# A larger fixed part for VectorE's instructions in the plan of the first attention, later inverses, and ScalarE's copies of the output projection behind the last exponential

## Chip, cores and metric

One core of one Trainium2 chip. The metric is the device time of one execution in microseconds (us); each kernel's time is the median of its runs.

## What is computed

Four layers follow one another on x of 2048 x 640 (float32): attention, a state-space convolution, attention again, the convolution again, each with a layer norm in front and the input added behind. Both attentions have the same weights, with 32 heads of 20 channels. Cut to what matters:

```python
def _A_ref(x, wqkv, wo):                     # H = 32, D = 640, S = 2048
    q, k, v = split(x @ wqkv)                # 32 heads of 20
    p = softmax(einsum("bhqd,bhkd->bhqk", q, k) * Dh ** -0.5)
    return merge(einsum("bhqk,bhkd->bhqd", p, v)) @ wo

def _B_ref(u, ...):                          # per channel, 128 states
    K = 2 Re(sum_n C[d, n] * exp(A[d, n] * dt[d] * pos))
    return causal_conv(u, K) + u * D_skip    # by FFT in the reference

x = x + _A_ref(layernorm(x)); x = x + _B_ref(layernorm(x))
x = x + _A_ref(layernorm(x)); x = x + _B_ref(layernorm(x))
```

## The kernel before

**Attention.** `attention` runs over 32 turns. A turn is a group g of four heads (8 groups) by a block qb of 512 queries (4 blocks), and it has 16 steps kt of 128 keys. In each step TensorE (PE) makes the scores of two pairs of heads (S, L858), ScalarE (ACT) takes their exponentials (pt, one instruction of 128 x 1024 for each pair, so 32 a turn and 1024 an attention), and `values` multiplies pt with V into two accumulators pa (L892). V has a column of ones, which gives the sums of the softmax. At the end of a turn VectorE (DVE) copies and adds pa to oc. PE needs that copy before it can write the next turn's pa. The sums of a block (number 4g + qb) go over DRAM: `sums` stores them (dn<-oc), `load` brings them back across all partitions (dr<-dn), `invert` takes 1/x on VectorE, `back` stores that (dn<-dr), and `spread` reads it for all rows (db<-dn). `scale` multiplies oc by db right behind the next turn's evacuation, and `store_block` writes the result (ot<-oc). These DMAs are issued by GpSimd (POOL).

**Work between the exponentials.** While the attention runs, PE and VectorE get other work. `jobs` is the projection of the next heads' q and k: units of 15 matrix products into the two banks m (L611), followed on VectorE by five instructions that `post` and its caller issue: qc (twice), sq, qhi, qlo. Two stores (qs or ks, on SP's queue) then send qhi and qlo to DRAM, from where `load_k` and `load_q` bring them into kop and qop, also on SP's queue. In the first attention there is also `kgen`, the filler: VectorE builds tables of the convolution's kernel K (expansions kpw, ktab, kwc, kwb, then products ka and kb), `contract` multiplies them on PE (m<-kb,ka, L329), VectorE empties that into ko, and kd<-ko stores it.

**What sets the order.** Instructions of an engine run in the order in which they are recorded, and `Plan` decides that order with modelled times for PE, ScalarE and VectorE. Every VectorE instruction is priced in `Ordered` (L77) at a fixed part of 0.07 us and one element per partition each 1/960 us. `weave` hands out filler as long as the planned time of VectorE is less than 0.2 us past that of PE. `emptied` plans when a bank is free, `slot` starts jobs by it, and `fill` does all of it once per exponential. A list `later` holds functions by planned time; the steps of a block's sums stand in it at fixed distances from the evacuation (L935), and with them the loads of the filler's powers (kpw<-wd). When filler and jobs are done, `end_jobs` frees their space and asks for the output weights wo and for x (SP); GpSimd splits the weights in two parts (woh and wol, L1169 and L1170).

**The end.** `out_proj` multiplies the stored blocks with wo, row tile by row tile. `Rows.split` copies a row tile to oh and VectorE takes the rest (ol). The first row tile's copy is VectorE's, the next ones are ScalarE's (CAST oh). `se.floor`, where it is set, ties ScalarE's later instructions behind a given one.

Of the kernel before, what the change touches and what calls it, by code (L numbers as in the profile page):

```python
# [50 lines left out]
class Plan:  # L51


    def __init__(self):
        self.pe = self.act = self.dve = 0.0
        self.keep = False

    def on_pe(self, cost, after=0.0):
        self.pe = max(self.pe, after) + cost
# [3 lines left out]
class Ordered:  # L63
# [5 lines left out]
    def __getattr__(self, name):  # L69
        f = getattr(self.engine, name)  # L70
        if name not in ("dma_start", "memset", "partition_all_reduce", "activation", "copy") and not self.count:
            return f

        def call(out, *a, **k):
            if self.count:
                big = a[0].shape if "reduce" in name else out.shape
                self.plan.dve = max(self.plan.dve, self.plan.pe - 0.9) + 0.07 + math.prod(big[1:]) / 960  # L77
            made = f(out, *a, **k)  # L78
            if self.plan.keep:
                self.last = self.tie(made, self.last)  # L80
            elif self.floor is not None:
                self.tie(made, self.floor)
            return made
        return call
# [3 lines left out]
def mha_s4d_kernel(ctx, tc, x_in, wqkv, wo, lar, aim, cr, ci, ldt, dsk,  # L88
                   c_e1, c_eb, c_f2, c_fa, c_sel, c_lv, c_id, c_sg, c_e16, c_f16, c_id16, c_dn, out, parts="asas", general=None):
    nc = tc.nc  # L90
    plan = Plan()
# [9 lines left out]
    se, ve, ge, sy = (Ordered(e, plan, tie, e is nc.vector) for e in (nc.scalar, nc.vector, nc.gpsimd, nc.sync))  # L101
# [87 lines left out]
    def chain(ins):  # L189
        last[0] = tie(ins, last[0])  # L190
# [208 lines left out]
    pend, slow = [], []  # L399
# [23 lines left out]
    def attention(x, stats):  # L423
        first_layer = stats is None
# [99 lines left out]
        sqs, outs, later, ends = [[], []], [], [], [0.0, 0.0]  # L524
# [318 lines left out]
        ends[:] = plan.pe, plan.pe  # L843
        sums_ = [plan.pe]
        se.last = ve.last = ge.last = sy.last = None
        plan.keep = True
        pp = c.enter_context(tc.tile_pool(name="pp", bufs=PB))
        ev = c.enter_context(tc.tile_pool(name="ev", bufs=2))
        ready, scaled, stored = [], [], {}
# [17 lines left out]
        def store_block(oc, blk):  # L867
            g, qb = divmod(blk, 4)
            for j in range(4):
                h = 4 * g + j  # L870
                ge.dma_start(ot[h * DH:(h + 1) * DH, 512 * qb:512 * qb + 512], oc[32 * j:32 * j + DH, :])
            stored[blk] = plan.pe

        def at_once(oc, blk):

            pb = pst("M", [P, 512], F32, tag="m0", name="m0")
            db = ev.tile([P, 512], F32, bufs=1, name="db")
            te.matmul(pb, dsel[0], oc, start=True, stop=True)
            ve.tensor_scalar_max(db, pb, 1e-30)
            ve.reciprocal(db, db)  # L880
            ve.tensor_mul(oc, oc, db)
            store_block(oc, blk)

        def values(qb, g, kt, pts, pa):

            V = Vt[g // 2 % 3]
            plan.on_pe(0.865)
            for r in range(2):
                rows = slice(64 * r, 64 * r + 64)
                for j in range(4):  # L890
                    h = 4 * (g % 2) + j
                    chain(te.matmul(pa[r][32 * j:32 * j + 32, :], V[rows, kt, VP * h:VP * h + 32],  # L892
                                    pts[j // 2][rows, 512 * (j % 2):512 * (j % 2) + 512],
                                    start=(kt == 0), stop=(kt == NI - 1), tile_position=(64 * r, 32 * j)))
            if kt == NI - 1:
                blk = 4 * g + qb
                oc = ev.tile([P, 512], F32, name="oc")
                dr = ev.tile([P, 16], F32, name="dr")
                db = []
                rows = dn[0, blk].rearrange("(j c) f -> j (c f)", j=4)  # L900
                plan.dve = max(plan.dve, plan.pe + 0.25)
                ve.tensor_copy(oc, pa[0])
                ve.tensor_add(oc, oc, pa[1])
                sums_[0] = plan.dve + 0.15
                while scaled:
                    scaled.pop(0)()
                if dsel and blk == NBK - 1:
                    later.append((plan.dve, lambda: at_once(oc, blk)))
                    return

                def sums():
                    for j in range(4):
                        ge.dma_start(rows[j:j + 1, :], oc[32 * j + DH:32 * j + DH + 1, :])

                def load():
                    ge.dma_start(dr, dn[0, blk])

                def invert():
                    ve.tensor_scalar_max(dr, dr, 1e-30)
                    ve.reciprocal(dr, dr)  # L920

                def back():
                    ge.dma_start(dn[1, blk], dr)

                def spread():
                    rows = dn[1, blk].rearrange("(j c) f -> j (c f)", j=4)
                    db.append(ev.tile([P, 512], F32, bufs=1, name="db"))
                    for j in range(4):
                        ge.dma_start(db[0][32 * j:32 * j + 32, :], rows[j:j + 1, :].to_broadcast([32, 512]))

                def scale():
                    ve.tensor_mul(oc, oc, db[0])
                    later.append((plan.dve + 0.3, lambda: store_block(oc, blk)))
                    later.sort(key=lambda e: e[0])
                later.extend((plan.dve + n, f) for n, f in (  # L935
                    (0.2, sums), (5.0, load), (10.0, invert), (11.0, back), (15.5, spread)))
                later.extend((plan.dve + n, lambda: slow and slow.pop(0)[1]()) for n in (18.0, 21.0, 24.0))
                if first_layer or g < H // 4 - 2:
                    scaled.append(scale)
                else:  # L940
                    later.append((plan.dve + 27.0, scale))
                later.sort(key=lambda e: e[0])
# [27 lines left out]
        def fill(j):  # L970

            if ready:
                t = max(ready[0][0] + 0.15, 0.0 if ready[0][3] else sums_[0])
                if t <= plan.pe + 0.1 or j and len(ready) > 2:
                    plan.on_pe(0.0, t)
                    values(*ready.pop(0)[1:])
            while slot(plan.act - 0.5):
                pass
            drain_later()
            weave()  # L980
# [146 lines left out]
        for r_ in ready:  # L1127
            values(*r_[1:])
# [11 lines left out]
            scaled.pop(0)()  # L1140
            drain_later(True)
        plan.keep = False
        se.floor = None if first_layer else se.last
        c.close()
        return *tail[:-1], rows, first

# [421 lines left out]
    def seq(x, general):  # L1568

        stats = None  # L1570
        for n in range(0, len(parts), 2):
            with ExitStack() as c:
                if general:
                    if stats is not None:
                        xpools.pop().__exit__(None, None, None)
                    attention_general(x)
                else:
                    x, wc, *tail = attention(x, stats)
                    rows = tail[2]
# [123 lines left out]
```

## Time and profile before

| | |
|---|---|
| median of 3 runs | 2681.47 us (2677.0 to 2681.95) |
| the profiled execution | 2680.85 us, span 2679.1 us |
| PE busy | 2530.0 us, 94% |
| ScalarE busy | 2368.7 us, 88% |
| VectorE busy | 1516.0 us, 57% |
| exponentials | 2048, each 1032 ns; they overlap |
| first exponential to the end of the last, first attention | 115.77 to 1101.84 us |
| the same, second attention | from 1491.2 us |

A row of the timeline has start and length in us, the engine, the line and operation, what is written <- what is read, the number of instructions, and in brackets the idle time in front with what ended it. The line L78 is the recording helper, so the tiles tell the instructions apart. SPq and POOLq rows are DMA issues. A row of stretches has the bounds, the length, and the busy time of PE, PE's weight loads, VectorE, ScalarE and GpSimd (with counts), then PE's granted clock, the DMA share and GB/s. A row of waits has who waited <- for whom: us in all, times, longest.

### The profile page before, as it was taken

The page shows a single profiled execution, that of the slowest core. Times are in us where ns is not written, and L with a number is a line of the kernel's source. Part 1 is how long each engine was busy: PE and PEld are TensorE (multiplying, and loading weights), DVE is VectorE, ACT ScalarE, POOL GpSimd, SP SyncE. Part 2 cuts the span into 40 slices and gives each one's busy share as a digit, 9 for nine tenths or more (in the row PEclk, how much of TensorE's full clock was granted, in tenths as well). Part 3 has the DMA queues.
Part 4 walks back from the last instruction along what each step waited for, and adds up shares of the span by engine and source line. Part 5 has one row for each costly group of instructions (what it writes and reads, how often), then busy time and mean ns, then how long its engine had stood idle before and what let it go on. Part 6 is the DMA issues. An engine that isn't in the chain of part 4 may idle for free.

```text
span 2679.1 us, 116332 instructions
## 1 busy us (share of the span) xinstructions
PE 2530.0 (94%) x51106; PEld 1425.0 (53%) x51106; DVE 1516.0 (57%) x3451; ACT 2368.7 (88%) x2793; POOL 827.7 (31%) x1256
## 2 busy tenths in 40 slices
PE   7899999999999998899998999999999998999898
PEld 3445444444444443678896444454444443444788
DVE  8687777886855994477776333232233221154865
ACT  7889999999999999676655799999999999999564
POOL 1123323333323334301672122222222222222376
PEclk9999999999999999999999999999999999999999
DMA  6513222322221224364542121121121113222465
GB/s 210 181 49 86 67 76 55 87 55 76 52 61 49 54 68 155 110 233 162 189 151 69 40 59 50 50 58 47 45 65 38 54 30 93 69 67 60 145 190 162
DMA packets 186580, 242.18 MB, mean 90 GB/s; under 512 B 43376, under 2 KB 128976, under 8 KB 184400
## 3 DMA queue, kind: packets, MB, share of 16 engines
q1 hardware_dynamic: 150048, 188.35, 21.8%
q0 software_dynamic: 36016, 46.30, 7.0%
q8 instruction: 403, 6.60, 1.0%
q14 instruction: 113, 0.93, 0.1%
HBM read 158.50 MB, written 76.01 MB: 88 GB/s over the span
## 4 chain that ended last, share of the span: by engine, by line
ACT 52%; PE 25%; issue 10%; DVE 6%; DMA 3%; POOL 1%; SPq 0%; ACTq 0%; DVEq 0%; POOLq 0%
ACT pt L78 50%; PE pa L892 4%; PE psv L1419 3%; PE psy L1429 3%; PE S L858 3%; PE psx L1407 2%; PE m L611 1%; PE psx L1384 1%; PE po L1312 1%; DMA kop<-ks 1%; PE pst L1394 1%; PE pkf L1272 1%; DVE ktab L78 1%; PE po L1307 1%; PE pq L764 1%
## 5 line engine op out<-in xcount | busy, mean ns | idle before, releaser
L78 ACT ACTIVATE pt<-S 128x1024 f32<-128x1024 f32 x2048 | 1928.6, 1032 | 41.4 <-PE S L858 29.2
L892 PE MATMUL pa<-pt,V 64*32 64x512 f32 x16384 | 1100.9, 590 | 1.4 <-DVE oc L78 1.2
L858 PE MATMUL S<-qop,kop 61*32 61x512 f16 x16384 | 882.9, 381 | 85.2 <-ACT pt L78 68.4
L858 PEld LDWEIGHTS <-kop 61*32 61x32 f16 x16384 | 366.7, 89 | 741.1 <-issue 622.4
L892 PEld LDWEIGHTS pa<-pt,V 64*32 64x32 f32 x16384 | 315.1, 106 | 74.6 <-issue 9.7
L78 POOL DMA_DIRECT2D dn<-oc x252 | 124.5, 501 | 670.6 <-DVE oc L78 643.8
L78 DVE TENSOR_SCALAR qc<-m 128x512 f32<-128x512 f32 (+1 forms) x68 | 46.8, 689 | 303.6 <-PE m L611 303.6
L78 POOL DMA_DIRECT2D db<-dn x252 | 128.0, 514 | 135.1 <-DMA dn<-dr 132.1
L78 DVE COPY oc<-pa 128x512 f32<-128x512 f32 x64 | 44.1, 690 | 199.6 <-PE pa L892 191.9
L611 PE MATMUL m<-xh,wh 64*32 64x512 f16 x2560 | 147.9, 379 | 5.5 <-DVE qc L78 5.5
L78 POOL DMA_DIRECT2D ot<-oc x256 | 130.4, 516 | 71.6 <-DVE oc L78 42.8
L611 PE MATMUL m<-xh,wl 64*32 64x512 f16 x2560 | 148.1, 377 | 0.0
L611 PE MATMUL m<-xl,wh 64*32 64x512 f16 x2560 | 146.7, 376 | 0.0
L611 PEld LDWEIGHTS <-wh 64*32 64x32 f16 x5120 | 92.9, 93 | 78.4 <-issue 36.4
L78 ACT COPY xt<-pst 128x1024 f16<-128x1024 f16 x80 | 81.6, 1022 | 47.2 <-PE pst L1394 47.0
L1412 POOL TENSOR_TENSOR t<-t,kb 128x512 f32<-128x512 f32 x80 | 102.0, 1276 | 67.6 <-DVE t L78 66.7
L78 POOL DMA_DIRECT2D dn<-dr x63 | 35.3, 560 | 248.8 <-DVE dr L78 236.4
L78 DVE TENSOR_SCALAR V<-m 128x160 f32<-128x160 f32 x64 | 20.7, 324 | 158.5 <-PE m L577 158.5
L78 DVE TENSOR_TENSOR kb<-ktab 128x512 f32<-128x512 f32 x160 | 107.7, 692 | 0.0
L577 PEld LDWEIGHTS <-xh 128*128 128x128 f16 x960 | 79.7, 98 | 47.0 <-issue 31.6
L1413 POOL TENSOR_TENSOR t<-t,t 128x512 f32<-128x512 f32 x78 | 99.3, 1273 | 8.5 <-DVE t L78 2.6
L329 PEld LDWEIGHTS m<-kb,ka 128*32 128x32 f32 x3840 | 61.0, 109 | 72.1 <-issue 55.3
(305 smaller groups left out, 4020.7 us busy)
## 6 DMA issues: line engine op xcount, KB each, us to landing
ka<-kha SPq DMA_DIRECT2D x80, 256.0 KB
kb<-khb SPq DMA_DIRECT2D x80, 256.0 KB
db<-dn POOLq DMA_DIRECT2D x252, 64.0 KB, 2.6
kop<-ks SPq DMA_DIRECT2D x176, 80.0 KB
kpw<-wd POOLq DMA_DIRECT2D x60, 192.0 KB, 4.7
qop<-qs SPq DMA_DIRECT2D x256, 40.0 KB
ot<-oc POOLq DMA_DIRECT2D x256, 40.0 KB, 3.0
kha<-kn SPq DMA_DIRECT2D x20, 512.0 KB
```

The costliest lines, as they stand in the source:

```text
L78: made = f(out, *a, **k)
L329: chain(te.matmul(ps[32 * j:32 * j + 32, c8, :], a[n][:, ch, :], b[n][:, dd, :], start=(n == 0), stop=(n == 2), tile_position=(0, 32 * j)))
L577: chain(te.matmul(ps[:, :n], a_[:, ct, sl], m[:, ct, :], start=(k == 0), stop=(k == 14)))
L611: chain(te.matmul(ps[r][32 * t:32 * t + 32, :], a_[rows, ct, 32 * u:32 * u + 32], m[rows, ct, 512 * v:512 * v + 512], start=(k == 0), stop ...
L764: te.matmul(pq, a_[:, ct, :], m[:, ct, sl], start=(n == 0), stop=(n == 14))
L858: chain(te.matmul(S[32 * t:32 * t + 32, 512 * r:512 * r + 512], kt_[rows, kc + 32 * t:kc + 32 * t + 32], qt[rows, :], start=True, stop=Tru ...
L892: chain(te.matmul(pa[r][32 * j:32 * j + 32, :], V[rows, kt, VP * h:VP * h + 32], pts[j // 2][rows, 512 * (j % 2):512 * (j % 2) + 512], sta ...
L1407: te.matmul(px, f2[:, f, :], xt[:, k, :], start=(n == 0), stop=(n == 2))
L1412: ge.tensor_mul(t2, t2, kb)
L1413: (ge if g0 else ve).tensor_add(t1, t1, t2)
L1419: te.matmul(pv[:, g].rearrange("p r i c -> p (r i c)"), t1[:, g * P:g * P + P], fa, start=True, stop=True)
L1429: te.matmul(py[:, i, :], eb[:, 4 * i4 + i, r, :], v[:, r, 4 * i4 + i].rearrange("p g c -> p (g c)"), start=(r == 0), stop=(r == 1))
```

## The change

```diff
@@ Plan, Ordered
-        self.keep = False
+        self.keep, self.fixed = False, 0.07
...
-                self.plan.dve = max(self.plan.dve, self.plan.pe - 0.9) + 0.07 + math.prod(big[1:]) / 960
+                self.plan.dve = max(self.plan.dve, self.plan.pe - 0.9) + self.plan.fixed + math.prod(big[1:]) / 960
@@ attention
-        plan.keep = True
+        plan.keep, plan.fixed = True, 0.11 if first_layer else 0.07
+        wait = 2.5 if first_layer else 0.0
...
-                    (0.2, sums), (5.0, load), (10.0, invert), (11.0, back), (15.5, spread)))
-                later.extend((plan.dve + n, lambda: slow and slow.pop(0)[1]()) for n in (18.0, 21.0, 24.0))
+                    (0.2, sums), (5.0, load), (10.0 + wait, invert), (11.0 + wait, back), (15.5 + wait, spread)))
+                later.extend((plan.dve + n, lambda: slow and slow.pop(0)[1]()) for n in (18.0 + wait, 21.0 + wait, 24.0 + wait))
...
-        se.floor = None if first_layer else se.last
+        se.floor = se.last
```

In the first attention the plan now counts 0.11 us for the fixed part of each VectorE instruction. The inverses of a block's sums, their way back, their spreading and the loads of powers stand 2.5 us of planned time later. ScalarE's instructions behind the attention are tied behind its last exponential, as they were in the second attention already. No instruction is added or taken away. In the changed kernel's rows lines behind L845 have a number one higher.

First place: VectorE at the start of turn 7, where turn 6's accumulators are emptied (oc<-pa). Before, the five rows of a unit of the projection (qc to qlo) stand right ahead of it:

```order
L78 TENSOR_TENSOR kb_7337<-ktab 128x512
L78 TENSOR_TENSOR kb_7338<-ktab,kdif 128x512
L78 TENSOR_SCALAR qc<-m_7061 128x512
L78 SCALAR_TENSOR_TENSOR qc<-m_7062,qc 128x512
L78 TENSOR_TENSOR sq<-qc 128x512
L78 CAST qhi<-qc 128x512
L78 TENSOR_TENSOR qlo<-qc,qhi 128x512
L78 COPY oc<-pa_6449 128x512
L78 TENSOR_TENSOR oc<-oc,pa_6450 128x512
L78 TENSOR_TENSOR oc<-oc,db 128x512
```

The same place of the changed kernel, where an expansion of the filler's tables (kpw, ktab, kwc) and one emptying of its bank (ko) stand there:

```order
L78 TENSOR_TENSOR kpw_166<-kpw_166 128x384
L78 COPY ktab<-kpw_166 128x32x3x2
L78 COPY ktab<-kpw_166 128x32x3
L78 COPY ktab<-k_ci 128x32
L78 TENSOR_TENSOR kwc_7311<-kpw_166,k_cr 128x96
L78 TENSOR_TENSOR kwc_7312<-kpw_166,k_ci 128x96
L78 TENSOR_SCALAR ko<-m_7275 128x128
L78 COPY oc<-pa_6469 128x512
L78 TENSOR_TENSOR oc<-oc,pa_6470 128x512
L78 TENSOR_TENSOR oc<-oc,db 128x512
```

The unit has moved away from the evacuation, and VectorE has less of the filler behind it at this point.

Second place: VectorE at the start of turn 8, the first of a new group of heads. Before:

```order
L78 TENSOR_SCALAR qc<-m_7955 128x512
L78 SCALAR_TENSOR_TENSOR qc<-m_7956,qc 128x512
L78 TENSOR_TENSOR sq<-qc 128x512
L78 CAST qhi<-qc 128x512
L78 TENSOR_TENSOR qlo<-qc,qhi 128x512
L78 COPY oc<-pa_7342 128x512
```

Now:

```order
L78 TENSOR_SCALAR qc<-m_7757 128x512
L78 SCALAR_TENSOR_TENSOR qc<-m_7758,qc 128x512
L78 TENSOR_TENSOR sq<-qc 128x512
L78 CAST qhi<-qc 128x512
L78 TENSOR_TENSOR qlo<-qc,qhi 128x512
L78 TENSOR_SCALAR ko<-m_8114 128x128
L78 TENSOR_TENSOR kat<-ktab 128x512
L78 TENSOR_TENSOR ka_8193<-ktab,kdif 128x512
L78 TENSOR_TENSOR ka_8194<-ktab 128x512
L78 COPY oc<-pa_7315 128x512
```

The unit now ends four rows ahead of the evacuation. On PE its last product stands six exponentials earlier, before the end of turn 7.

Third place: the end of the attention on GpSimd, from the evacuation rows of one block (dn<-oc, ot<-oc) over its sums (dr<-dn, dn<-dr, db<-dn) to the next block's. Before, the splitting of the output weights (woh, wol) stands between the load and the way back of block 28's sums:

```order
L78 DMA dr<-dn 128x16
L1169 CAST woh<-wot 128x640 x2
L1170 ISA
L1170 TENSOR_TENSOR wol<-wot,woh 128x640 x2
L1169 CAST woh<-wot 128x640 x2
L1170 TENSOR_TENSOR wol<-wot,woh 128x640 x2
L1169 CAST woh<-wot 128x640
L1170 TENSOR_TENSOR wol<-wot,woh 128x640
L78 DMA dn<-dr 128x16
L78 DMA db<-dn 32x512 x4
L78 DMA kd<-ko 128x8x64
L78 DMA dn<-oc 16x1x32 x4
```

Now it stands between those of block 29, with the last store of K among it:

```order
L78 DMA dr<-dn 128x16
L1170 CAST woh<-wot 128x640 x2
L1171 ISA
L1171 TENSOR_TENSOR wol<-wot,woh 128x640 x2
L1170 CAST woh<-wot 128x640 x2
L1171 TENSOR_TENSOR wol<-wot,woh 128x640 x2
L78 DMA kd<-ko 128x8x64
L78 DMA dn<-dr 128x16
L1170 CAST woh<-wot 128x640
L1171 TENSOR_TENSOR wol<-wot,woh 128x640
L78 DMA db<-dn 32x512 x4
L78 DMA dn<-oc 16x1x32 x4
```

The splitting has moved one turn towards the end. On SP the loads of the weights and of all of x now stand behind the last loads of q. On ScalarE the first CAST oh, which stood behind 1000 exponentials, stands behind all 1024.

## The prediction, made before the changed kernel ran

> **What bounds the kernel now.** I read the page first, then the busy times by stretch, then what ScalarE waited for.
>
> ```profile
> span 2679.1 us, 116332 instructions
> ACT 52%; PE 25%; issue 10%; DVE 6%; DMA 3%; POOL 1%; SPq 0%; ACTq 0%; DVEq 0%; POOLq 0%
> ```
>
> The chain that ended last runs mostly over ScalarE (ACT): the exponentials of the two attentions set the time. The profiled execution took 2680.85 us, 1.75 more than its span and 0.62 under the median of 2681.47; what the trace can save I take off the median as it is. Behind the last rows of the first attention the order of instructions is the same in both kernels on all engines, and so it is on TensorE (PE) and VectorE (DVE) up to about 146 us. What can change lies between, in 31 of the 32 turns of the first attention (a turn is 32 exponentials).
>
> Stretches of it, with their length and the busy us of PE, PE's loads, DVE, ACT and POOL:
>
> ```profile
> 150.00:865.05 715.05, 698.04 (x18437) 345.39 (x18436) 530.27 (x1132) 700.38 (x744) 233.21 (x399) 1.00 0.25 66
> 865.05:1011.00 145.95, 133.69 (x3480) 59.60 (x3473) 134.54 (x303) 145.92 (x158) 53.06 (x87) 1.00 0.24 61
> 1011.00:1072.00 61.00, 52.72 (x1224) 22.56 (x1231) 22.93 (x39) 59.68 (x65) 27.58 (x39) 1.00 0.50 167
> ```
>
> From 865 to 1011 ScalarE hardly rests, though VectorE is busy for 134.54 of 145.95 us with the filler: filler there is free. From 150 to 865 ScalarE rests for 715.05 - 700.38 = 14.7 us. PE is busy for 698.04 of that stretch, which leaves it 17 us in 24 turns, 0.7 a turn: what holds PE up soon reaches ScalarE. The waits of ScalarE from 150 us to its last exponential, and its longest undisturbed run:
>
> ```profile
> ACT pt L78 <- PE S L858: 12.5, 15, 1.9
> 864.77 158.27 ACT L78 ACTIVATE pt<-S 128x1024 f32<-128x1024 f32 x170
> ```
>
> So 12.5 us in 15 waits is nearly all that the plan can win; 158.27 / 170 = 0.931 us is an exponential's pace, 29.8 us a turn. ScalarE's timeline shows where they lie (the bracket is the idle time before a run):
>
> ```profile
> 190.29 30.17 ACT L78 ACTIVATE pt<-S 128x1024 f32<-128x1024 f32 x32 [1.93 <-PE S L858]
> ...
> 300.73 11.56 ACT L78 ACTIVATE pt<-S 128x1024 f32<-128x1024 f32 x12 [0.84 <-PE S L858]
> ...
> 342.71 2.11 ACT L78 ACTIVATE pt<-S 128x1024 f32<-128x1024 f32 x2 [1.13 <-PE S L858]
> 345.91 25.61 ACT L78 ACTIVATE pt<-S 128x1024 f32<-128x1024 f32 x27 [1.09 <-PE S L858]
> 372.77 15.64 ACT L78 ACTIVATE pt<-S 128x1024 f32<-128x1024 f32 x16 [1.25 <-PE S L858]
> 389.75 48.14 ACT L78 ACTIVATE pt<-S 128x1024 f32<-128x1024 f32 x51 [1.34 <-PE S L858]
> 438.36 2.11 ACT L78 ACTIVATE pt<-S 128x1024 f32<-128x1024 f32 x2 [0.47 <-PE S L858]
> 441.56 104.25 ACT L78 ACTIVATE pt<-S 128x1024 f32<-128x1024 f32 x111 [1.09 <-PE S L858]
> 546.24 71.54 ACT L78 ACTIVATE pt<-S 128x1024 f32<-128x1024 f32 x76 [0.43 <-PE S L858]
> 618.40 218.31 ACT L78 ACTIVATE pt<-S 128x1024 f32<-128x1024 f32 x229 [0.62 <-PE S L858]
> 837.47 28.32 ACT L78 ACTIVATE pt<-S 128x1024 f32<-128x1024 f32 x30 [0.76 <-PE S L858]
> ```
>
> **The change part by part. First, 0.11 for 0.07.** How good is the plan's price? Two stretches of VectorE without a pause; the first is an expansion of K's tables (first and last row of 18 instructions, then the copy behind them, and PE, which waits for that copy):
>
> ```profile
> 179.88 0.27 DVE L78 TENSOR_TENSOR kwc<-kpw,k_ci 128x96 f32<-128x96 f32 x1
> ...
> 186.75 0.69 DVE L78 TENSOR_TENSOR kat<-ktab 128x512 f32<-128x512 f32 x1
> 187.35 0.68 DVE L78 COPY oc<-pa 128x512 f32<-128x512 f32 x1
> 188.09 1.43 PE L892 MATMUL pa<-pt,V 64*32 64x512 f32 x12 [1.02 <-DVE oc L78]
> ```
>
> The 18 instructions have 9 x 96 + 6 x 288 + 896 + 2 x 512 = 4512 elements, 4.70 us at the plan's 960 a microsecond. They took 187.35 - 179.88 = 7.47, so the fixed part was 2.77 / 18 = 0.154 us each. The old plan gave 5.96 and ran 1.5 us ahead of the chip, the new one gives 6.68 and runs 0.8 ahead. The second is a unit of the next heads' projection, the five instructions on qc, with the evacuation of a finished block (oc) right behind:
>
> ```profile
> 339.79 0.68 DVE L78 TENSOR_SCALAR qc<-m 128x512 f32<-128x512 f32 x1
> ...
> 342.98 0.68 DVE L78 COPY oc<-pa 128x512 f32<-128x512 f32 x1
> ...
> 346.17 0.68 DVE L78 TENSOR_TENSOR kb<-ktab,kdif 128x512 f32<-128x512 f32 x1
> 346.77 0.69 DVE L78 TENSOR_TENSOR kb<-ktab 128x512 f32<-128x512 f32 x1
> 343.71 1.43 PE L892 MATMUL pa<-pt,V 64*32 64x512 f32 x12
> ```
>
> Five instructions in 342.98 - 339.79 = 3.19 us; the plan said 3.02 and will say 3.22, fixed part 0.105. Two kb stand 0.60 apart: 0.533 + 0.067, where 0.11 is too much. The Trainium skill ("Perfetto Trace Analysis", section "Optimizing Scalar/DVE Operations") gives about 60 ns for VectorE on SBUF and 125 ns on PSUM; the kb rows agree, the expansion and the qc chain, whose instructions wait for one another's results, do not. By that page 0.07 was right for SBUF, the first term below would be nothing and the sum 1.2 us smaller.
>
> An overpriced kb costs filler: some 48 in a turn by 0.04 is 1.9 us of planned time. Hence the filler ends later: its last four kb and two ko rows stand behind turn 30's first evacuation, where before none did. That is hidden, by the rows from 865 to 1011, and ends with more than a turn to spare.
>
> Terms, by the ScalarE rows above:
> - 190.29 (1.93): VectorE was late from the expansion in front of it, which stays there. Its lateness goes from 1.5 to 0.8, so I take 1.2 of the 1.93.
> - 300.73 (0.84) and 546.24 (0.43): filler and qc late. I take 1.0 together.
> - 342.71 and 345.91 (2.22), 438.36 and 441.56 (1.56): the 3.2 us qc chain stands right ahead of oc, so that PE gets its accumulator back only at 343.7, as the row shows. By the order, turn 7's evacuation no longer has it there (first place in the part on the change), nor has turn 10's. I take 3.4 of 3.78.
> - 837.47 (0.76): the same collision at turn 23, in both orders. Nothing.
> - 372.77 and 618.40: turns 8 and 16 begin before their K and Q are loaded; those loads go when the old halves come free. Nothing.
> - 389.75 (1.34): the second half of K for turn 8 went out late, behind a store that waited for qlo on SP's queue:
>
> ```profile
> 374.14 1.20 SPq L78 DMA_DIRECT2D qs<-qlo  x1
> 375.44 2.30 SPq L78 DMA_DIRECT2D kop<-ks  x4
> 389.22 0.41 PE L858 MATMUL S<-qop,kop 61*32 61x512 f16 x7 [1.34 <-DMA kop<-ks]
> ```
>
> In the new order this unit is finished four filler rows earlier against oc (second place), and on PE six exponentials earlier, 5.6 us; the store, still ahead of the loads, waits no more. I take 1.3.
>
> **Second, the 2.5 us** for inverses, their way back, spreading, and the loads of powers. VectorE's waits for a block's sums in the whole first attention:
>
> ```profile
> DVE dr L78 <- DMA dr<-dn: 31.9, 11, 8.9
> ```
>
> Of 31 inverses 11 waited, the long ones while VectorE had nothing else, and none stands ahead of a row of the list above. How soon a spread lands, from the page (KB, us to landing):
>
> ```profile
> db<-dn POOLq DMA_DIRECT2D x252, 64.0 KB, 2.6
> ```
>
> The spread is planned 18.0 us behind oc in place of 15.5 and lands 2.6 later, of a turn of 29.8. I take nothing; bounds: 0.5 saved, 0.5 lost.
>
> **Third, ScalarE's floor.** One copy stood 24 exponentials ahead of the end:
>
> ```profile
> 1079.11 0.73 ACT L78 CAST oh<-otl 128x640 fp32r<-128x640 f32 x1
> 1079.72 22.11 ACT L78 ACTIVATE pt<-S 128x1024 f32<-128x1024 f32 x24
> 1104.99 0.82 DVE L78 TENSOR_TENSOR ol<-otl,oh 128x640 fp32r<-128x640 f32 x1
> ```
>
> It takes 1079.72 - 1079.11 = 0.6 us from the exponentials: saved. Behind the last one it ends near 1102.6, and its reader, ol, starts at 1104.99 behind oc anyway: 2.4 us of cover. The next copy waits for PE, as before.
>
> Sum: 1.2 + 1.0 + 3.4 + 1.3 + 0.6 = 7.5. Against it I set 1.0 for new collisions, one as the smaller ones in the list, since units now end elsewhere in 20 turns. Net 6.5: **2681.47 - 6.5 = 2675.0 us**.
>
> **Rivals.** *The waits only move.* PE's 0.7 us a turn stay, and any chain of 3.2 us may meet an evacuation or a K load. Of the five blocks of before with qc right ahead of oc two cost 2.22 and 1.56, one 0.76, and two nothing of their own; in the new order one such block is left, and two have one or two rows between, as before. If these come to 5.5, the net is 2: 2679.5.
>
> *Slower: POOL's copies of the output weights in the way of the last blocks.* They stood behind turn 28's sums and now stand behind turn 29's (third place), a turn later:
>
> ```profile
> 1015.13 2.27 SPq L78 DMA_DIRECT2D wot<-in_wo  x5
> 1021.28 1.99 POOL L1169 CAST woh<-wot 128x640 fp32r<-128x640 f32 x2
> ...
> 1040.82 0.74 POOL L78 DMA_DIRECT2D dn<-dr  x1
> ...
> 1085.05 2.01 POOL L78 DMA_DIRECT2D db<-dn  x4 [2.79 <-DMA dn<-dr]
> 1104.39 0.69 DVE L78 TENSOR_TENSOR oc<-oc,db 128x512 f32<-128x512 f32 x1
> ```
>
> The copies ran from 1021.28, 6 us after their data were asked for, to 1040.82. One turn later that is 1051 to 1071. Block 30's round over DRAM, from 1075 to the landing of db near 1090, then keeps its time, for a use at 1104.39. Against it: the weights (1.6 MB) and x (5.2 MB) are now asked for together; at the 167 GB/s of the stretch from 1011 that is 41 us. Were the copies to wait for all of it, they would be 35 us later and end at 1106; block 30's round would end 17 us behind that, at 1123, VectorE would stand at oc with PE's results queued behind it, 19 us lost and 6.5 won: 2694. It decides from 16 us of delay; from 28 on the kernel is slower by what can be told. For it speaks only that the queue is shared; the weights are asked for first.
>
> *The price is too high and the filler spills over the end.* The order excludes it, as said.
>
> **How the numbers follow.** Forecast 0.54 (own range 2670 to 2676), waits only move 0.39 (2676 to 2682), slower 0.07. A measurement of this kernel can tell about 0.2%, 5.4 us, so the same chances hold for faster, same and slower. The range goes from 2668 (all of 12.5 + 0.6 won) to 2683 (nothing won and two waits more).
>
> **What would show it.** Right: the ScalarE rows near 190, 342, 390 and 440 without their brackets, 1024 exponentials without a break, filler up to 1050. Wrong: waits for PE between 150 and 865 that sum to over 9 us, at other turns; or VectorE idle before the last oc.

## The result, and the profile after

| | median, us | runs | from, to |
|---|---|---|---|
| before | 2678.84 | 7 | 2676.94 to 2681.95 |
| changed | 2670.49 | 7 | 2668.27 to 2673.94 |

The ratio is 0.9969, with a 95% interval of 0.9957 to 0.998: the change saves 8.35 us (5.4 to 11.5). Forecast were 6.5 us and 2675.0 us, taken off the 2681.47 us of the three runs known then. The profiled execution took 2672.17 us.

The head of the page and its chain that ended last look much as before; ScalarE has 58% of the chain where it had 52%:

```profile
span 2670.4 us, 116325 instructions
ACT 58%; PE 21%; issue 11%; DVE 3%; DMA 2%; POOL 1%; SPq 0%; ACTq 0%; POOLq 0%; DVEq 0%
```

All of it lies in the first attention: from its first exponential to the start of its last one it took 984.99 us before and 976.37 now, 8.62 less. The part between the attentions (390.46, 391.17), the second attention (979.19, 979.28) and the end (208.65, 208.78) are as they were. The first of the prediction's three stretches, where nearly all of ScalarE's rest was:

```profile
150.00:865.05 715.05, 700.10 (x18557) 343.70 (x18557) 534.17 (x1140) 706.47 (x752) 237.85 (x408) 1.00 0.25 67
```

From 150 to 865 ScalarE was busy 700.38 us and is now 706.47, so its rest fell from 14.7 to 8.6. Its waits for scores from 150 us to the last exponential were 12.5 us in 15; now (us, times, longest):

```profile
ACT pt L78 <- PE S L859: 6.1, 7, 3.0
```

ScalarE's timeline says where these seven are, and what became of the eleven rows that the prediction listed:

```profile
139.03 224.86 ACT L78 ACTIVATE pt<-S 128x1024 f32<-128x1024 f32 x239 [0.93 <-PE S L859]
366.88 1.02 ACT L78 ACTIVATE pt<-S 128x1024 f32<-128x1024 f32 x1 [2.99 <-PE S L859]
368.36 1.02 ACT L78 ACTIVATE pt<-S 128x1024 f32<-128x1024 f32 x1 [0.46 <-PE S L859]
370.17 31.96 ACT L78 ACTIVATE pt<-S 128x1024 f32<-128x1024 f32 x34 [0.78 <-PE S L859]
402.59 425.75 ACT L78 ACTIVATE pt<-S 128x1024 f32<-128x1024 f32 x449 [0.46 <-PE S L859]
829.10 144.35 ACT L78 ACTIVATE pt<-S 128x1024 f32<-128x1024 f32 x155 [0.76 <-PE S L859]
973.82 99.72 ACT L78 ACTIVATE pt<-S 128x1024 f32<-128x1024 f32 x107 [0.37 <-PE S L859]
1073.81 18.44 ACT L78 ACTIVATE pt<-S 128x1024 f32<-128x1024 f32 x20 [0.27 <-PE S L859]
1092.07 0.78 ACT L78 CAST oh<-otl 128x640 fp32r<-128x640 f32 x1
```

One run of 239 exponentials covers what was broken near 190, 300 and 342, and one of 449 what was broken near 438, 546 and 618. The wait at turn 23 (837.47 before, 829.10 now) is the same 0.76. The copy stands behind the last exponential. One thing got worse: the start of turn 8 waits 2.99 + 0.46 + 0.78 = 4.23 us, where it had waited 1.25.

What PE waits for there, and what SP's queue does ahead of it (in the rows of waits: us in all, times, longest):

```profile
363.66 0.37 PE L859 MATMUL S<-qop,kop 61*32 61x512 f16 x1 [0.45 <-DMA qop<-qm]
366.35 0.41 PE L859 MATMUL S<-qop,kop 61*32 61x512 f16 x7 [2.32 <-DMA qs<-qlo]
```

```profile
347.90 0.32 SPq L78 DMA_DIRECT2D qs<-qhi  x1
348.63 0.32 SPq L78 DMA_DIRECT2D qs<-qlo  x1
349.04 2.31 SPq L78 DMA_DIRECT2D kop<-ks  x4
```

```profile
SPq L78 <- DVE qhi L78: 18.2, 1, 18.2
```

SP stands for 18.2 us at a store of qhi, which VectorE makes at 347.45 to 347.87. The loads of K and Q for turn 8 are behind that store, and they go at 349.04, the moment it is out. The second and third of the three waits, 1.24 us together, lie in a stretch from 367.3 to 370.7 us in which PE's granted clock was 0.50; in the rest of the time from 150 to 865 us it was 1.00, and in the trace of before it was 1.00 throughout.

### The profile page after: what moved, and what is told of

Read it like the earlier page. It is cut to its first block, busy times and chain, and to the rows that moved or that the text cites. A ratio compares the mean times of both kernels' runs of the same rounds, so it can differ in the third digit from the quotient of the medians.

```text
span 2670.4 us, 116325 instructions
## 1 busy us (share of the span) xinstructions
PE 2528.2 (95%) x51106; PEld 1424.3 (53%) x51106; DVE 1511.7 (57%) x3451; ACT 2368.0 (89%) x2793; POOL 824.4 (31%) x1256
## 4 chain that ended last, share of the span: by engine, by line
ACT 58%; PE 21%; issue 11%; DVE 3%; DMA 2%; POOL 1%; SPq 0%; ACTq 0%; POOLq 0%; DVEq 0%
ACT pt L78 56%; PE psv L1420 3%; PE psy L1430 3%; PE pa L893 2%; PE psx L1408 2%; PE S L859 2%; PE psx L1385 1%; PE po L1313 1%; PE pst L1395 1%; PE pkf L1273 1%; PE m L611 1%; PE po L1308 1%; PE pq L764 1%; PE pkx L1257 1%; PE pkt L1265 1%
## 5 line engine op out<-in xcount | busy, mean ns | idle before, releaser
L78 ACT COPY xt<-pst 128x1024 f16<-128x1024 f16 x80 | 81.6, 1023 | 47.2 <-PE pst L1395 46.7
```

## The experiments

Each run is compared with runs of the kernel before on the same chip: 2680.3 us for the first four, 2680.09 for the next four, 2680.61 for the last four. Intervals are at 95%.

**e1: the price alone.** 0.11 is in, the 2.5 us and the floor are not.

```diff
-        wait = 2.5 if first_layer else 0.0
+        wait = 0.0
...
-        se.floor = se.last
+        se.floor = None if first_layer else se.last
```

> Only the fixed part of 0.11; inverses and ScalarE's copy as before. If the gain is the price's (theory of the prediction): ScalarE's waits for PE from 150 us to its last exponential fall from 12.5 to about 6, as in the changed kernel, and the time is 7 to 8 us under before, near 2671. If the 2.5 us of delay are needed to win it (rival): less than half of that, 2675 or more.

Measured: 2686.01 us, ratio 1.0019 (1.001 to 1.0028), 5.7 us slower than before. Neither outcome had that. In the trace the waits for scores up to the copy come to 7.1 us, near the 6.1 of the changed kernel. The loss stands at ScalarE's copy, which without the floor lies in front of the last 24 exponentials:

```profile
1049.57 21.38 ACT L78 ACTIVATE pt<-S 128x1024 f32<-128x1024 f32 x23
1083.01 0.72 ACT L78 CAST oh<-otl 128x640 fp32r<-128x640 f32 x1 [12.06 <-DMA otl<-ot]
...
1088.51 1.94 ACT L78 ACTIVATE pt<-S 128x1024 f32<-128x1024 f32 x2 [1.11 <-PE S L859]
1091.01 16.61 ACT L78 ACTIVATE pt<-S 128x1024 f32<-128x1024 f32 x18 [0.56 <-PE S L859]
```

SP's queue shows why the load is late:

```profile
1066.12 0.38 SPq L78 DMA_DIRECT2D otl<-ot  x1
...
1068.08 1.69 SPq L78 DMA_DIRECT2D otl<-ot  x1
```

The filler ends a turn later under the new price, and with it the splitting of the output weights on GpSimd. SP's waits from 1040 to 1075 us say that it stood 6.3 us at the first otl for wol; the second otl then goes behind three loads of x (1280 KB each, 1066.55), and the DMA engines' share is 1.01 from 1070 to 1075 us. Before, SP did not wait for wol, and both loads went at 1059.15, 20 us ahead of the copy; here the copy's turn comes at 1071, 5 and 3 us behind them. It waits 12.06 us, and with the two waits behind it 13.7 us are lost on ScalarE.

**e2: the 2.5 us alone,** on the old price of 0.07, without the floor.

```diff
-        plan.keep, plan.fixed = True, 0.11 if first_layer else 0.07
+        plan.keep, plan.fixed = True, 0.07
...
-        se.floor = se.last
+        se.floor = None if first_layer else se.last
```

> Only the inverses, their way back, the spreading and the loads of powers 2.5 us later; the price stays 0.07. Theory of the prediction: nothing, within 2 us of before, and ScalarE's waits near 12. Rival (inverses that wait for their sums make VectorE late): 3 to 4 us faster. A third view, that any other order scatters the collisions anew: the waits lie at other turns and sum to anything between 6 and 16.

Measured: 2687.9 us, ratio 1.0026 (1.0017 to 1.0035), 7.6 us slower, which none of the three outcomes had. The waits for scores grow to some 20 us, and many lie elsewhere. The largest, with two small ones behind it 5.15 in all, is at the start of turn 12:

```profile
498.07 1.02 ACT L78 ACTIVATE pt<-S 128x1024 f32<-128x1024 f32 x1 [3.70 <-PE S L859]
```

and SP's waits from 470 to 500 us say that it is the same store ahead of the loads:

```profile
SPq L78 <- DVE qhi L78: 19.0, 1, 19.0
```

**e3: the floor alone,** on the old price.

```diff
-        plan.keep, plan.fixed = True, 0.11 if first_layer else 0.07
-        wait = 2.5 if first_layer else 0.0
+        plan.keep, plan.fixed = True, 0.07
+        wait = 0.0
```

> Only the copy behind the last exponential. All engines but ScalarE have the order of before. The exponentials run without the 0.6 us pause 24 before the end, and the first product of the output projection starts no later behind the last exponential: 0.6 us less, too little for one time to show, so the rows are read. Rival: the copy's reader on VectorE is now late and the 0.6 us are given back within 10 us.

Measured: 2677.66 us, one run, 0.5 us under the lowest of before's 21 on that chip; one run can't show 0.6 us. In the rows the copy stands behind the last exponential, and the pause 24 exponentials ahead of the end is gone. ScalarE's waits are at the places of before, and their sizes show how far a wait varies with the same order: 0.70 us at turn 8's start, 0.16 at turn 16's and 0.75 near 1027, where before's trace has 1.25, 0.62 and 1.27 in two.

**h_hold: the changed kernel, with stores kept from standing ahead of the loads.** At a change of heads a unit's stores stay off SP's queue until the loads of K and Q stand on it. Four pairs of stores move behind loads; the order on all other engines is that of the changed kernel.

```diff
-            while outs and (end or outs[0][0] <= plan.pe):
+            while outs and (end or not hold[0] and outs[0][0] <= plan.pe):
...
+                hold[0] = first_layer and (kt >= 6 and g2 != g or kt <= 1 and n > 0 and turns[n - 1][0] != g)
```

> The changed kernel, but in a group's last turn from step 7 on and up to the next turn's second step, stores of a projection's unit wait until the loads of K are out; only SP's queue has another order. In the changed kernel the loads for turn 8 went out 2 us late behind such a store and ScalarE waits 4.2 us at that turn's start. Theory: they go out 2 us earlier and 2 to 4 us of the 4.2 go: 2667 to 2669. Rival: the 4.2 us come from stores and a load of weights that share the way with the last loads of K and Q, issued 361 to 363; then nothing changes, 2671.

Measured: 2666.64 us, ratio 0.9952 (0.9939 to 0.9966). The interval overlaps that of the change, so the trace decides: the first attention takes 972.20 us in place of 976.37, and the wait at turn 8 is gone.

```profile
142.78 258.72 ACT L78 ACTIVATE pt<-S 128x1024 f32<-128x1024 f32 x275 [0.76 <-PE S L861]
401.96 425.56 ACT L78 ACTIVATE pt<-S 128x1024 f32<-128x1024 f32 x449 [0.47 <-PE S L861]
```

SP's queue and its waits there:

```profile
349.72 2.30 SPq L78 DMA_DIRECT2D kop<-ks  x4
...
362.36 0.35 SPq L78 DMA_DIRECT2D qs<-qhi  x1
```

```profile
SPq L78 <- PE S L861: 17.2, 3, 16.0
```

The times of the rows mislead here: 349.72 is later than 349.04. But the whole attention of this execution runs 3.75 us later (142.78 against 139.03 at the same exponential); counted from the exponentials the loads go 3.1 us earlier. And ahead of these loads SP now waits for PE, 16.0 us until the old half of K is free, and no more for VectorE.

**e4: price and floor without the 2.5 us.**

```diff
-        wait = 2.5 if first_layer else 0.0
+        wait = 0.0
```

> The change without its 2.5 us (price 0.11 and the floor are in, the inverses, spreads and loads of powers stand where they did). Theory: with the price in, the 2.5 us is worth next to nothing; ScalarE's order is that of the changed kernel, and the price-alone run had the same waits but for one of 1.21 us near turn 20 and its 12 us pause at the end, which the floor takes away: 2671.5 us (2670 to 2673.5), and a wait of about 1.2 us near 730. Rival: the 2.5 us carries a part of its own, so that without it a third or more of the 8.35 us is lost: 2673.5 to 2677, in several new waits. Since the wait alone was 7.6 us slower on the old price, a third outcome is that it is better without: below 2669.

Measured: 2672.82 us, ratio 0.9972 (0.9962 to 0.9982), as the changed kernel within what the runs can tell. In the trace ScalarE's waits come to 5.4 us against 6.1; there is a new one of 1.10 at 514 and one of 0.62 near 733. From e1 it differs by the floor alone, and the two are 13.2 us apart, with intervals that don't meet.

**b_hold: the kernel before with the stores held back,** nothing else; four pairs of stores move on SP's queue. The edit is that of h_hold.

> The kernel before, and at a change of heads the unit's stores on SP's queue are held back until the K and Q loads of the new heads stand on it; four pairs of stores move behind loads, nothing else. Theory (a store that waits for VectorE's qhi or qlo holds the loads behind it on SP's in-order queue): the waits of before at 372.77 (1.25), 389.75 (1.34) and 618.40 (0.62) go, 3.2 us: 2677.1 against 2680.3. Rival, as the prediction had it for two of the three (the loads go when the old halves come free, the store is no part of it): only 389.75 goes, 1.3 us: 2679.0, and the other two stay in the rows.

Measured: 2679.17 us, ratio 0.9996 (0.9987 to 1.0005). The times can't tell 3.2 from 1.3 us; the trace can. The first attention takes 982.50 us against 984.99. Its rows around turns 8 and 16:

```profile
343.98 30.35 ACT L78 ACTIVATE pt<-S 128x1024 f32<-128x1024 f32 x32 [1.09 <-PE S L860]
375.05 58.67 ACT L78 ACTIVATE pt<-S 128x1024 f32<-128x1024 f32 x62 [0.71 <-PE S L860]
...
614.00 218.50 ACT L78 ACTIVATE pt<-S 128x1024 f32<-128x1024 f32 x229 [0.31 <-PE S L860]
```

The run that broke off after 27 exponentials before, at turn 8's start, goes on to 32, and the wait at the second half of K is gone. A new one of 0.71 has come six exponentials into turn 8: there the five rows of qc stand right ahead of block 7's evacuation (372.11), and before, the wait for the loads had hidden what that costs. So the two waits of turn 8 hung on stores ahead of loads, but only 2.2 of the 3.2 us are left as a gain. For turn 16 nothing is shown: 0.31 is left of 0.62, and e3, with the stores where they were, has 0.16.

**q009: h_hold with 0.09.**

```diff
-        plan.keep, plan.fixed = True, 0.11 if first_layer else 0.07
+        plan.keep, plan.fixed = True, 0.09 if first_layer else 0.07
```

> The changed kernel with the stores held back (2666.6 in an earlier run) and 0.09 in place of 0.11. Theory (what counts is how many evacuations have the five rows of qc right in front of them, not how near the price is to VectorE's durations): two such blocks more than with 0.11, 1.0 to 1.7 us each: 2668.5 to 2670. Rival (the nearer to the measured durations, the better, step by step): half way between the old and the new price is half of what the price brings, some 6 us: 2672 to 2674.

Measured: 2670.28 us, ratio 0.9963 (0.9949 to 0.9976). Of the waits that 0.11 doesn't have, the largest, 2.4 us, stand at the two blocks that got their qc rows back in front of the evacuation, 13 and 14:

```profile
547.74 2.11 ACT L78 ACTIVATE pt<-S 128x1024 f32<-128x1024 f32 x2 [0.51 <-PE S L861]
550.93 30.21 ACT L78 ACTIVATE pt<-S 128x1024 f32<-128x1024 f32 x32 [1.09 <-PE S L861]
581.92 243.83 ACT L78 ACTIVATE pt<-S 128x1024 f32<-128x1024 f32 x256 [0.78 <-PE S L861]
```

**q013: h_hold with 0.13.** The edit is the same line.

> The changed kernel with the stores held back (2666.6 in an earlier run) and 0.13 in place of 0.11. Theory (number of evacuations with qc right in front): three such blocks against two with 0.11, at others than before, and less lateness left behind the expansions: 2666 to 2669. Rival (a price over the measured 0.105 of the qc chain spaces the filler out and costs): filler ends later still, and the time goes up by more than 3 us: 2670 to 2674.

Measured: 2703.85 us, ratio 1.0091 (1.0078 to 1.0105): 24 us slower than before. Neither theory had that size. Most of it is one wait; the others come to 11.7 us, against 2.0 in h_hold:

```profile
1094.56 1.02 ACT L78 ACTIVATE pt<-S 128x1024 f32<-128x1024 f32 x1 [30.34 <-PE S L861]
```

The code does all filler that is left ahead of the last turn (`need(*every)` at turn 31). At 0.13 that is 96 matrix products of the filler in one piece on PE, waiting for VectorE. The groups from 1060 to 1097, on PE (the trace has two records for each of these products, so the piece is 192 of the 216; 24 lie ahead of it):

```profile
L329 PE MATMUL m<-kb,ka 128*32 128x64 f32 x216 | 7.9, 303 | 22.8 <-DVE kb L78 22.8
```

**q007: h_hold with the old 0.07;** the 2.5 us and the floor stay.

> The changed kernel with the stores held back (2666.6 in an earlier run), and the price put back from 0.11 to 0.07; the 2.5 us and the floor stay. Theory (the price is the part that wins; without it eight evacuations again have the five rows of qc right in front, and the expansions run late): the wait-alone run had some 20 us of waits and 2687.9; less the waits at the starts of turns 8, 12 and 16, some 8 us, and the floor at nothing: 2680 (2677 to 2683). Rival (with the stores held back most of the price's win is there already): 2671 or less.

Measured: 2679.93 us, ratio 0.9995 (0.9986 to 1.0004). Against h_hold the price alone is worth 12 to 13 us. The waits for scores are back:

```profile
ACT pt L78 <- PE S L861: 11.6, 15, 1.9
```

**c_small: h_hold, priced by kind,** 0.15 for instructions of at most 320 elements, 0.07 for the others.

```diff
-  self.plan.fixed + math.prod(big[1:]) / 960
+  (self.plan.small if math.prod(big[1:]) <= 320 else self.plan.fixed) + math.prod(big[1:]) / 960
...
-        plan.keep, plan.fixed = True, 0.11 if first_layer else 0.07
+        plan.keep, plan.fixed, plan.small = True, 0.07, 0.15 if first_layer else 0.07
```

> The same kernel with the stores held back, priced by kind: 0.15 for VectorE's instructions of at most 320 elements (the expansions), 0.07 for all others, as the trace of before has them (0.154 and 0.067). Theory (the old price's error lies in the small instructions that wait for one another; flat 0.11 is right on the sum and so gives the same places): 2666 to 2668, waits of ScalarE under 3 us from 150 us on. Rival (flat 0.11 wins because it spaces the long instructions out, the qc chain and kb): with those back at 0.07 the waits come back: 2673 or more.

Measured: 2665.62 us, ratio 0.994 (0.9926 to 0.9953), as h_hold within what can be told; waits of ScalarE 2.4 us. The long instructions keep 0.07 and the gain is there. So it is enough to price the small ones higher. Which of them matter, the expansions or others of at most 320 elements such as ko, this run does not tell.

**q0105: h_hold with 0.105.**

> The same kernel with the stores held back and 0.105 in place of 0.11, the fixed part that the qc chain showed. Theory (evacuations with qc right in front): one row more between qc and the evacuation of block 22, so the wait of 0.75 us there may go, the rest as it was: 2666 (2665 to 2667.5). Rival (the time moves with the price itself, steadily): the same within 1 us of 0.11, with the wait of 0.75 us still there.

Measured: 2663.93 us, ratio 0.9934 (0.9921 to 0.9948), 16.7 us faster than before: the fastest version here, beyond the interval of the change and 1 us under the range of its theory. Not only the wait behind block 22 is gone; from 141.84 us on the first attention has none that the timeline shows:

```profile
141.84 945.63 ACT L78 ACTIVATE pt<-S 128x1024 f32<-128x1024 f32 x1005 [0.44 <-PE S L861]
```

**q0115: h_hold with 0.115.**

> The same kernel with the stores held back and 0.115. At 0.13 the rest of the filler, 96 matmuls of it in one piece, stood ahead of the last turn and cost 30.3 us; at 0.115 it is 36 matmuls. Theory (whatever is left of the filler is done ahead of the last turn at VectorE's pace): 30.3 x 36 / 96 = 11 us there, and four evacuations with qc in front instead of two, some 2 us: 2680 (2675 to 2682). Rival (VectorE has the operands of a short rest ready by then, so only a long one costs): no pause there, 2667 to 2670.

Measured: 2678.74 us, ratio 0.9993 (0.9984 to 1.0002). The rest of the filler ahead of the last turn costs 8.38 us, then 3.32:

```profile
1065.17 1.02 ACT L78 ACTIVATE pt<-S 128x1024 f32<-128x1024 f32 x1 [8.38 <-PE S L861]
1069.51 1.02 ACT L78 ACTIVATE pt<-S 128x1024 f32<-128x1024 f32 x1 [3.32 <-PE S L861]
```

Together 11.7, where 11 had been worked out from 0.13. That agreement is luck: the 8.38 stand ahead of 12 products and the 3.32 ahead of the other 36, and by the rows VectorE is late for the 12 because its instructions ran beside GpSimd's splitting of the weights: from 1050.64 to 1062.70 it needed 12.1 us for six that take 3.5 us where GpSimd is not in the way (worked out from their usual steps in these traces).

## Why the prediction was right, step by step

The forecast direction and the main mechanism held, and the sum of 6.5 was near the measured 8.35. Its terms, against ScalarE's rows of before and after:

| step | forecast | measured |
|---|---|---|
| 190.29, expansion late | 1.2 | 1.93 |
| 300.73 and 546.24 | 1.0 | 1.27 |
| qc ahead of oc, turns 7 and 10 | 3.4 | 3.78 |
| 389.75, second half of K | 1.3 | 1.34 |
| 837.47 | 0 | 0 |
| 372.77, turn 8's start | 0 | -2.98 (1.25 to 4.23) |
| 618.40, turn 16's start | 0 | 0.62 |
| not named: 220 and 312, 1023 and 1029 | 0 | 0.33 and 1.27 |
| the copy in front of the end | 0.6 | 0.6 |
| new waits (402, 973, 1073) | -1.0 | -1.10 |
| sum | 6.5 | 7.06 |

Of the trace's 8.62 us another 0.44 lie in turn 0; the last 1.1 are in gaps that the timeline doesn't list. Part of the nearness is luck: the waits that were named gave 1.4 us more than forecast, others that were not named 2.2, and turn 8 took 3.0 back. Rows of half a microsecond are within what e3 shows a wait to vary by.

- **The price works through the places of the evacuations.** Shown by q007, q009, h_hold and q0105, where nothing but the price differs: their traces have 6, 3, 1 and 0 evacuations with the qc rows right in front. The count does not go on falling with the price: q0115 has 4 and q013 3. In q007 5.2 of the 11.6 us of waits stand behind four of the six, 1.9 behind the late expansion near 190, and 4.6 elsewhere, so qc in front is the largest part and not all. That a higher price for instructions of at most 320 elements is enough is shown by c_small; that they are late because each waits for the one before it is argued from the rows of the expansion. This bears on what the prediction weighed against the Trainium skill ("Perfetto Trace Analysis", "Optimizing Scalar/DVE Operations"): its 60 ns are near the 0.067 of the long instructions, and with them at 0.07 and 0.15 for the small ones the gain stays.
- **190.29 was mis-sized, by a wrong reason.** The prediction had the expansion stay in front of the evacuation and only its lateness shrink from 1.5 to 0.8. It doesn't stay whole. VectorE after:

```profile
182.85 0.83 DVE L78 TENSOR_TENSOR kwb<-ktab 128x288 f32<-128x288 f32 x2
183.78 0.69 DVE L78 COPY oc<-pa 128x512 f32<-128x512 f32 x1
...
185.79 0.45 DVE L78 TENSOR_TENSOR ktab<-kwb,kwb 128x288 f32<-128x288 f32 x1
...
187.88 0.69 DVE L78 TENSOR_TENSOR kat<-ktab 128x512 f32<-128x512 f32 x1
```

  Its last four rows, from ktab at 185.79 to kat's end 2.8 us later, stand behind the evacuation. The whole 1.93 went.
- **"372.77 and 618.40: those loads go when the old halves come free. Nothing" is the step that failed.** At turn 8 they went when a store in front of them on SP's queue had its data. SP's queue before:

```profile
354.69 0.32 SPq L78 DMA_DIRECT2D qs<-qhi  x1
355.42 0.32 SPq L78 DMA_DIRECT2D qs<-qlo  x1
355.83 2.30 SPq L78 DMA_DIRECT2D kop<-ks  x4
```

  The prediction saw this for 389.75 and not for the first half. b_hold shows the cause on the kernel before and h_hold on the changed one: with the stores held back the loads go 2.4 and 3.1 us earlier, counted from the same exponential, and the wait at turn 8's start is gone; in the changed kernel that gains 4.2 us. For turn 16 it is not shown.
- **Why turn 8's wait grew from 1.25 to 4.23 us is open.** It is not the store: counted from the same exponential, the loads begin only 0.7 us later than before and end 0.2 us later. The unit whose earlier end put the second half right is another one, with its stores at 361.82. Two things stand beside the wait in the trace. From 357.47 us on GpSimd asks for three loads of powers (kpw<-wd, 192 KB each) where it asked for one before, and from 360 to 362 us the DMA engines' share is 0.94, where it was 0.28 at the same distance from the exponentials. And behind PE's pauses of 0.45 and 2.32 us comes the stretch at a granted clock of 0.50, with 1.24 of the 4.23 us. In e4 PE pauses for 2.10 and 0.57 us at this place, the clock stays at 1.00, and ScalarE waits 2.88 us in all. No run takes these apart.
- **The 2.5 us: no difference on the new price that e4 can tell** (2672.82 and 2670.49, intervals overlapping); whether it lies within the bounds of 0.5 is too fine for these runs. On the old price alone it was 7.6 us slower (e2), far outside the bounds. Its place in the sum was right only because the price had been changed with it; 5.15 us of e2 are the start of turn 12, where a store stands ahead of the loads, and q007, with stores held back and the floor, is 8 us faster than e2.
- **The floor's 0.6 was read against the kernel before, and that is what was left out.** On the old price the rows of e3 agree with it. With the new price the floor is what keeps 13 us from being lost (e1 against e4): the splitting of the weights stands a turn later, the loads of otl wait for it and go 5 and 3 us ahead of the copy in place of 20, and the copy in front of the last 24 exponentials would wait for them. The prediction followed GpSimd's copies into that later turn and not SP's otl behind them.
- **The slower rival came as worked out, short of its price.** GpSimd's copies moved behind turn 29's sums and delayed those of block 29. GpSimd and VectorE after:

```profile
1041.87 1.39 POOL L1170 CAST woh<-wot 128x640 fp32r<-128x640 f32 x2
...
1062.49 2.03 POOL L78 DMA_DIRECT2D db<-dn  x4
...
1084.86 2.02 POOL L78 DMA_DIRECT2D db<-dn  x4 [1.60 <-DMA dn<-dr]
```

```profile
1072.42 0.69 DVE L78 TENSOR_TENSOR oc<-oc,db 128x512 f32<-128x512 f32 x1 [7.06 <-DMA db<-dn]
...
1094.80 0.69 DVE L78 TENSOR_TENSOR oc<-oc,db 128x512 f32<-128x512 f32 x1
```

  VectorE waited 7.06 us for block 29's db with nothing of PE's behind it; block 30's went out at 1084.86, and its reader at 1094.80 waited for nothing. The copies started 5 us after their data were asked for, as before, so the shared queue did them no harm.
- **"The price is too high" was rightly left out for 0.11, with a wrong margin.** The filler must be done by the start of turn 31, not by the end: the last copy of a bank of its (ko) is at 1044.23 in the changed kernel's trace, and turn 31 begins near 1062, so the spare was some 18 us, not more than a turn. Already 0.115 spends it (q0115), where GpSimd's splitting, now beside the filler's last instructions, adds to the loss; 0.13 is 24 us slower than before. 0.11 is near the edge.

Open, besides turn 8: whether the 2.5 us is worth one or two microseconds with the new price, in either direction; and what of e2's loss beyond turn 12 comes from which block.

## What to carry to other kernels

A planner's price matters where it is systematically off for one kind of instruction, and it pays in steps, by which neighbours meet; look at the places, not at the mean error, and look how far the next cliff is. A DMA queue that runs in order is an engine like the others: whatever waits there for data holds the loads behind it, and an engine's idle row names the load, not the store that held it. A term read from the trace of before can be a guard in the kernel after: ask of each part of a change what the other parts move towards it.

## What the runs showed of the hardware

VectorE's instructions with two inputs were stretched several times over while GpSimd split the output weights. In q013, VectorE and GpSimd from 1074 us on:

```profile
1077.86 3.82 DVE L78 TENSOR_TENSOR ka<-ktab,kdif 128x512 f32<-128x512 f32 x1
...
1082.83 4.07 DVE L78 TENSOR_TENSOR ka<-ka,ka 128x512 f32<-128x512 f32 x1
```

```profile
1078.11 3.01 POOL L1174 TENSOR_TENSOR wol<-wot,woh 128x640 fp32r<-128x640 f32 x2
...
1083.34 3.01 POOL L1174 TENSOR_TENSOR wol<-wot,woh 128x640 fp32r<-128x640 f32 x2
```

The same instruction takes 0.69 us elsewhere in that trace; here it ends some 0.6 us behind the second wol, as if it had started only then. This lengthens the rest of the filler just where it is waited for. The Trainium skill ("SBUF — State Buffer", section "SBUF: two separate sides") says that VectorE with two SBUF inputs and GpSimd share a port pair under an exclusive lock, the loser blocked for the whole instruction; these rows agree. They also look as if a VectorE instruction can be passed over for two GpSimd instructions in a row: each of the two began, by its row, before the pair of wol and ended behind both.

PE's granted clock fell to 0.50 behind some of its pauses in the attention and not behind others. In the changed kernel it did so from 367.3 to 370.7 us, behind pauses of 0.45 and 2.32 us, and a row of eight products for scores took 1.00 us where such a row takes 0.41 elsewhere; in e4, behind pauses of 2.10 and 0.57 us at the same place, it stayed at 1.00.
